# Attention into a GELU MLP on one core: weighted sums two units at a time, with 64-row products for the half blocks

## The chip, the cores and the metric

The kernel runs on one NeuronCore of one Trainium2 chip. The metric is the device time of one execution in microseconds (us); smaller is better. Engines are named as in the profile: PE is TensorE's matmul, PEld its weight load, DVE VectorE, ACT ScalarE, POOL GpSimd, SP the queue that issues the DMAs.

## The reference

Eight batches of eight heads, 576 positions of 64 features, with a causal window of 128 and a linear bias, followed by a two-layer MLP on the 4608 tokens:

```
scores = q @ k.T / sqrt(64) + bias        # (8, 8, 576, 576), only 0 <= i - j < 128 counts
attn   = softmax(scores)
x      = (attn @ v) as (4608, 512)        # "weighted sums"
out    = gelu(x @ w_in) @ w_out           # 512 -> 2048 -> 512, float32 result
```

Every matrix product keeps float32 precision by splitting each operand into two float16 parts (high and low) and adding three products: high*high, high*low, low*high.

## The kernel before

**Units.** The attention works on units: one batch `b` and one pair of heads `hp`, so 4 units a batch and 32 in all. A unit has 9 query blocks of 64 queries. Query block `j` sees the key blocks `j-2`, `j-1` and `j` (64 keys each, 192 keys).

**Stages of a unit.** `scores` (line 496) computes the scores with 54 products of 64 rows and 64 output rows; `biased` (548) scales them on DVE and adds the bias; `softmax` (633) takes maxima on DVE, exponentials on ACT and writes normalised weights (high part by POOL, low part by DVE in `low_weights`, 652) into the one buffer `e_main`; two transposing DMAs from SP's queue (line 658) turn them into the tile `et`, keys on partitions. `et` has two buffers, `et0` for units 0 and 2 and `et1` for units 1 and 3 of a batch.

**Weighted sums.** `weigh` (675) multiplies v by the weights. A 128-key block `kb` of v is the stationary operand (64 columns, one head), and `et` is the moving one, two query blocks (128 columns) at a time where both lie in the same part. For every even query block the block `kb = j/2` holds only 64 keys that count, and for every odd one the block `kb = (j-3)/2` does; the other 64 rows of such a product are zeros. Head 0 writes partitions 0 to 63 and head 1 partitions 64 to 127 of one PSUM bank, so two products stand side by side in the array. The MLP runs on tiles of 512 tokens, which don't end where batches end (576 tokens), so a unit's 9 query blocks fall into two parts (`blocks_of`, 670): part 0 goes to MLP tile `b`, part 1 to tile `b+1`, each in a bank of its own. `leave` (708) brings a part out of PSUM: ACT writes the high float16 part to the tile `x` (line 720), DVE the low part (line 721, shown as the helper's line 218).

**Order of the work.** The first three batches (0 to 2) follow an order written out by hand. Batches 3 to 7 are computed inside the loop over MLP tiles `t = 2` to 6 (line 1250), with `b = t + 1`. Each tile has 32 steps: in steps 0 to 15 `mlp_in` (12 products of 128x128 by 512 columns, line 747) and `gelu`, in steps 16 to 31 12 products of `mlp_out` (line 793) each, with `put` after every fourth. After these products a step may also start the scores of a unit (steps 2, 11, 16, 21) or weigh one (steps 12, 20, 30, 30):

```
SCORES_AT, WEIGH_AT = (2, 11, 16, 21), (12, 20, 30, 30)
```

In tile 2 the first scores come at step 4 and the first weighing at step 13; in tile 6 the last scores come at step 22. A scheduler that simulates the engines orders each engine's instructions from this program order; PE follows it in the trace.

**PSUM.** Eight banks: four under the tag `mm` (MLP products, and the score banks that begin with group 4 or 7) and four under `att` (the other three banks of a unit's scores, and the banks `av` of the weighted sums). A bank is reused once its readers on DVE and ACT are done.

## Time and profile before

| | us |
|---|---|
| median of 3 runs | 880.12 |
| lowest and highest of them | 879.17, 880.38 |
| the profiled execution | 879.11 |
| its span in the profile | 877.3 |

The profiled execution has its own time, and a span (first to last instruction) that is 1.8 us shorter. In the rows, a group of instructions has its line in the kernel, its engine, output and inputs, the shape (array rows * columns, then partitions x elements) and a count. In a timeline the first column is the start in us from the span's start, the second the time from the first start to the last end; since products overlap, the price of a group is better read from its start to the start of the next group.

### The profile page before, as it was taken

What the parts mean: (1) busy time and instruction counts of PE and PEld (TensorE: products, weight loads), DVE (VectorE), ACT (ScalarE), POOL (GpSimd) and SP (SyncE); (2) the same over time, 40 slices, a digit from 0 to 9 for tenths busy, and PEclk for the clock granted to TensorE, in tenths of its full rate; (3) what the DMA queues carried; (4) which work ended last, traced back from release to release, by engine and by line L of the source; (5) the groups of instructions that cost most, each with busy time, mean ns of one, the idle gap of its engine ahead of it and who ended that gap; (6) DMA issues with size and microseconds to landing.
All of it is one profiled execution on the core that took longest, in us unless ns stands there. A gap on an engine that the chain in (4) does not pass through costs nothing.

```text
span 877.3 us, 18582 instructions
## 1 busy us (share of the span) xinstructions
PE 861.7 (98%) x7428; PEld 476.9 (54%) x7428; DVE 709.3 (81%) x1388; ACT 546.5 (62%) x1147; POOL 196.0 (22%) x412
## 2 busy tenths in 40 slices
PE   6999999999999999999999999999999999999998
PEld 4644445544554545454545545445545554588887
DVE  6999999999768984887578775878477889998871
ACT  8999879896755573465464455466355338644760
POOL 0011000222015440452126421543054310000000
PEclk9999999999999999999999999999999999999999
DMA  9766645452572346233622473225122330001001
GB/s 311 268 208 230 228 117 133 134 168 62 132 233 38 73 97 203 57 69 77 187 72 56 93 171 117 55 55 118 39 56 56 78 67 13 0 13 37 1 1 49
DMA packets 174598, 91.63 MB, mean 104 GB/s; under 512 B 133680, under 2 KB 156336, under 8 KB 174384
## 3 DMA queue, kind: packets, MB, share of 16 engines
q1 hardware_dynamic: 174512, 90.45, 38.3%
q8 instruction: 58, 0.95, 0.4%
q14 instruction: 28, 0.23, 0.1%
HBM read 46.53 MB, written 9.44 MB: 64 GB/s over the span
## 4 chain that ended last, share of the span: by engine, by line
PE 70%; DVE 12%; ACT 2%; DMA 2%; issue 2%; POOL 1%; SPq 0%; ACTq 0%; POOLq 0%; DVEq 0%
PE h L747 27%; PE o L793 24%; PE av L700 4%; PE u_out L1082 4%; PE sc L529 3%; PE u L995 2%; DVE e_main L218 2%; DMA et<-e_main 2%; PE v L995 2%; DVE nmax L638 1%; DVE s L555 1%; PE z_out L1082 1%; PE x_out L1082 1%; PE y_out L1082 1%; PE v_out L1082 1%
## 5 line engine op out<-in xcount | busy, mean ns | idle before, releaser
L747 PE MATMUL h<-x,wi 128*128 128x512 f16 x1536 | 337.7, 379 | 1.1 <-ACT g L769 0.6
L747 PEld LDWEIGHTS <-wi 128*128 128x128 f16 x1536 | 148.5, 98 | 181.2 <-issue 4.0
L793 PE MATMUL o<-wo,g 128*128 128x512 f16 x864 | 192.4, 379 | 0.0
L793 PEld LDWEIGHTS <-g 128*128 128x128 f16 x1152 | 110.9, 98 | 132.8 <-issue 0.3
L641 ACT ACTIVATE s<-s,nmax 128x192 f32<-128x192 f32 x252 | 110.8, 441 | 46.3 <-DVE nmax L638 46.1
L218 DVE SCALAR_TENSOR_TENSOR e_main<-s,z,e_main 128x192 f16<-128x192 f32 x252 | 116.3, 505 | 15.2 <-POOL e_main L650 10.4
L771 POOL TENSOR_SCALAR g<-g,sg 128x512 f16<-128x512 f32 x96 | 76.8, 806 | 228.0 <-ACT g L769 200.8
L769 ACT ACTIVATE g<-h,gs 128x512 f32<-128x512 f32 x96 | 64.0, 686 | 95.9 <-PE h L747 59.1
L218 DVE SCALAR_TENSOR_TENSOR g<-g,sg,g 128x512 f16<-128x512 f32 x96 | 80.1, 851 | 34.0 <-POOL g L771 33.8
L650 POOL TENSOR_SCALAR e_main<-s,z 128x192 f16<-128x192 f32 x180 | 89.1, 514 | 66.9 <-ACT s L641 37.9
L555 DVE SCALAR_TENSOR_TENSOR s<-sc,cs,bias_h 128x384 f32<-128x384 f32 x112 | 64.2, 608 | 10.1 <-PE sc L529 9.9
L793 PE MATMUL o<-wo_first,g 128*128 128x512 f16 x288 | 65.9, 379 | 0.0
L720 ACT ACTIVATE x<-av,cx 128x448 f16<-128x448 f32 (+6 forms) x52 | 24.3, 481 | 62.0 <-PE av L700 59.5
L790 PE MATMUL o<-zo,g 128*128 128x512 f32 x128 | 57.0, 597 | 0.0
L638 DVE TENSOR_REDUCE nmax<-s 128x5 f32<-128x960 f32 (+1 forms) x56 | 56.6, 1043 | 0.4 <-POOL s L561 0.3
L529 PE MATMUL sc<-kbuf,qbuf 64*64 64x192 f16 (+3 forms) x1656 | 48.3, 250 | 7.6 <-ACT qbuf L431 4.4
L561 POOL MEMSET s<- 64x128 f32 (+1 forms) x112 | 19.2, 172 | 142.3 <-DVE s L555 131.2
L218 DVE SCALAR_TENSOR_TENSOR x<-av,cx,x 128x448 f16<-128x448 f32 (+6 forms) x52 | 24.7, 493 | 28.5 <-ACT x L720 28.4
L641 ACT ACTIVATION_READ_ACCUMULATOR s<-s,nmax 128x1 f32 x252 | 47.1, 187 | 0.0
L700 PEld LDWEIGHTS <-vbuf 128*64 128x64 f16 x1680 | 40.4, 111 | 9.4 <-issue 8.8
L700 PE MATMUL av<-et,vbuf 128*64 128x128 f16 (+1 forms) x1680 | 42.7, 210 | 0.4 <-DMA et<-e_main 0.3
L1082 PEld LDWEIGHTS <-g 128*128 128x128 f16 x384 | 37.6, 98 | 4.6
(269 smaller groups left out, 1126.3 us busy)
## 6 DMA issues: line engine op xcount, KB each, us to landing
v<-vp SPq DMA_DIRECT2D x32, 320.0 KB, 5.2
out<-ob SPq DMA_DIRECT2D x34, 256.0 KB, 2.2
raw<-w_in SPq DMA_DIRECT2D x8, 1024.0 KB, 11.0
raw<-w_out SPq DMA_DIRECT2D x8, 1024.0 KB, 6.7
q<-qp SPq DMA_DIRECT2D x7, 1152.0 KB, 6.0
k<-kp SPq DMA_DIRECT2D x7, 1152.0 KB, 7.5
qbuf<-qp SPq DMA_DIRECT2D x4, 288.0 KB, 5.4
kbuf<-kp SPq DMA_DIRECT2D x4, 288.0 KB, 5.7
```

The lines of the kernel that those rows point to most:

```text
L218: return nc.vector.scalar_tensor_tensor(out=dst, in0=src, scalar=scale, in1=high, op0=ALU.mult, op1=ALU.subtract)
L529: done = nc.tensor.matmul(ps[bank][o, n, gap:W], a, m[:, gap:W], start=(i == 0 and (n == 0 or b > 0)), stop=(i == len(terms) - 1 and b > 0 ...
L555: yield nc.vector.scalar_tensor_tensor(out=s[:, bank[0] : bank[0] + k, :], in0=ps[bank][:, 0:k, 0:W], scalar=cs, in1=bias.broadcast_to([P, ...
L638: yield nc.vector.tensor_reduce(out=nmax[:, r], in_=s[:, r], axis=AX.X, op=ALU.max, negate=True)
L641: yield nc.scalar.activation(s[:, i, :], s[:, i, :], AF.Exp, bias=nmax[:, i : i + 1], accum_out=z[:, i : i + 1])
L650: yield nc.gpsimd.tensor_scalar(e[:, i, 0, c], s[:, i], z[:, i : i + 1], 1.0, op0=ALU.mult, op1=ALU.mult)
L700: done = nc.tensor.matmul(av[r, (j - blocks[0]) * QB : (j - blocks[0] + len(js)) * QB], v32s[b][:, hp, kb, r] if b < EXACT else vbuf[:, vi ...
L747: done = nc.tensor.matmul(ph, wi[n][:, a, cc, k * P : (k + 1) * P], x[:, cc, b, :], start=(i == 0), stop=(i == 3 * NCC - 1),)
L769: yield nc.scalar.activation(g32, ph, AF.Gelu, scale=gsc[t, n])
L771: yield nc.gpsimd.tensor_scalar(g[:, r, 0], g32, gsg[t, n], 1.0, op0=ALU.mult, op1=ALU.mult)
L793: done = nc.tensor.matmul(o, g[:, r, a, c], wo[n][:, b, k, :], start=(fc == first and i == 0), stop=(fc == last and i == 2),)
L1082: nc.tensor.matmul(ps[name][:, tb], f(d, a)[:, k, tb * P : (tb + 1) * P], w(d, b, k), start=first, stop=True, skip_group_check=True,)
```

## The change

For batches 3 to 7, two units are weighed together: units 0 and 1 after step 18, units 2 and 3 after step 30 (no shift in tile 2 any more). `weigh_two` computes the half blocks as products of 64 rows, rows 0 to 63 for even query blocks (`low`) and rows 64 to 127 for odd ones (`high`), one query block (64 columns) a product, two `low` and two `high` in turn; then the whole 128-row blocks, again one query block a product. Even and odd query blocks of a part go to banks of their own, each bank holding both units: up to four `av` banks at once, from `att`. PE's order within it is fixed as written. `leave_two` brings out bank by bank: ACT both units in one instruction, DVE one instruction for each unit.

```diff
@@ new, beside weigh @@
+    def parity_blocks(b, part, odd):
+        return [j for j in blocks_of(b, part) if j % 2 == odd]
+
+    def weigh_two(one, two):
+        b, pair = one.b, (one, two)
+        k = 1 if b < EXACT else 2
+        banks = [(part, odd) for part in range(2) for odd in range(2) if parity_blocks(b, part, odd)]
+        for part, odd in banks:
+            one.av[part, odd] = bank_of([P, TT], "att" if b else "mm", f"av{one.u}_{b + part}_{odd}")
...
+        def job(rows, st, u, h, vi, ei, kb, slot, j):
+            part, odd, n = where[j]
+            g = 4 if j == 8 else (NEVEN if odd else 0) + 2 * h + j // 4
+            half = h if j == 8 else half_of(b, h, j)
+            c = slice(h * D, h * D + D)
+            at = (u * len(parity_blocks(b, part, odd)) + n) * QB
...
+                (part, odd, h), one.av[part, odd][c, at : at + QB],
+                v32s[b][rows, st.hp, kb, c] if b < EXACT else vbuf[rows, vi, st.hp, kb, c],
+                st.et[rows, (g * k + ei) * 2 + slot, half * QB : half * QB + QB],
...
+        terms = ((None, 0),) if b < EXACT else ((0, 0), (0, 1), (1, 0))
+        each = [(st, u, t) for u, st in enumerate(pair) for t in terms]
+        low = [(st, u, t, j // 2, 1, j) for st, u, t in each for j in range(0, NB, 2)]
+        high = [(st, u, t, (j - 3) // 2, 0, j) for st, u, t in each for j in range(3, NB, 2)]
+        for n, (st, u, t, *at) in enumerate(low):
+            for h in range(2):
+                job(slice(0, D), st, u, h, *t, *at)
+            if n < len(high):
+                st, u, t, *at = high[n]
+                for h in range(2):
+                    job(slice(D, P), st, u, h, *t, *at)
+        for st, u, t in each:
+            for j in range(1, NB):
+                for h in range(2):
+                    job(slice(0, P), st, u, h, *t, (j - 1) // 2, j % 2, j)
...
+            done = nc.tensor.matmul(o, a, m, start=key not in started, stop=left[key] == 0, skip_group_check=True)
...
+    def leave_two(one, two):
...
+        for part in range(2):
+            t = b + part
+            for odd in range(2):
+                js = parity_blocks(b, part, odd)
...
+                av = one.av[part, odd][:, 0 : 2 * n * QB].rearrange("p (u n k) -> p u n k", u=2, n=n)
...
+                yield nc.scalar.activation(dst(0, (0, 1)), av, AF.Copy, scale=c)
+                for u in range(2):
+                    yield low_part(dst(1, (u,)), av[:, u], c, dst(0, (u,)))
@@ the loop over tiles @@
-    SCORES_AT, WEIGH_AT = (2, 11, 16, 21), (12, 20, 30, 30)
+    SCORES_AT, WEIGH_AT = (2, 11, 16, 21), (18, 30)
...
-            scores_at[0], weigh_at[0] = scores_at[0] + 2, weigh_at[0] + 1
+            scores_at[0] += 2
...
-            for hp in range(NPAIR):
-                if weigh_at[hp] == step:
-                    for part in range(2):
-                        run(weigh(unit(b, hp), [part]))
-                        run(leave(unit(b, hp), [part]))
+            if step in WEIGH_AT:
+                two = [unit(b, 2 * WEIGH_AT.index(step) + n) for n in range(2)]
+                with tc.manual_schedule(engines={mybir.EngineType.PE}):
+                    run(weigh_two(*two))
+                run(leave_two(*two))
```

## Rows read from the trace of the kernel before

**Rows 1.** The page's busy times: PE, share of the span, instructions.

```profile
PE 861.7 (98%) x7428; PEld 476.9 (54%) x7428; DVE 709.3 (81%) x1388; ACT 546.5 (62%) x1147; POOL 196.0 (22%) x412
```

**Rows 2.** Stretches: one MLP tile (t = 3); columns: length, busy us by engine, PEclk.

```profile
344.60:438.86 94.26, 94.26 (x818) 46.89 (x817) 70.98 (x151) 50.33 (x112) 33.02 (x68) 1.00 0.42 101
```

**Rows 3.** Waits of PE, 250 to 725 us: total, times, longest.

```profile
PE h L747 <- ACT g L769: 0.6, 1, 0.6
```

**Rows 4.** Timeline of PE, batches 3 and 4: start, length, group, count.

```profile
310.00 1.60 PE L700 MATMUL av<-et,vbuf 128*64 128x128 f16 x66
311.53 2.76 PE L793 MATMUL o<-wo,g 128*128 128x512 f16 x12
...
339.06 3.00 PE L700 MATMUL av<-et,vbuf 128*64 128x128 f16 x132
342.00 2.76 PE L793 MATMUL o<-wo,g 128*128 128x512 f16 x12
...
380.99 1.55 PE L700 MATMUL av<-et,vbuf 128*64 128x128 f16 x54
382.47 7.94 PE L747 MATMUL h<-x,wi 128*128 128x512 f16 x36
...
417.77 7.93 PE L793 MATMUL o<-wo,g 128*128 128x512 f16 x36
...
428.13 5.34 PE L793 MATMUL o<-wo,g 128*128 128x512 f16 x24
433.41 2.91 PE L700 MATMUL av<-et,vbuf 128*64 128x128 f16 x108
436.25 2.76 PE L793 MATMUL o<-wo,g 128*128 128x512 f16 x12
```

**Rows 5.** Line 700's products, 309.9 to 311.5 and 380.9 to 382.4, by shape.

```profile
L700 PE MATMUL av<-et,vbuf x66: 192/196/243, 310.0 to 311.4; 128*64 128x64 f16 x36, 128*64 128x128 f16 x30
...
L700 PE MATMUL av<-et,vbuf x54: 192/219/243, 381.0 to 382.3; 128*64 128x128 f16 x42, 128*64 128x64 f16 x12
```

**Rows 6.** Weight loads begun by 433.43, 433.45 (line 700); 446.74, 446.76 (line 529).

```profile
433.41 0.11 PEld L700 LDWEIGHTS <-vbuf 128*64 128x64 f16 x2 [0.42 <-issue]
...
433.41 0.14 PEld L700 LDWEIGHTS <-vbuf 128*64 128x64 f16 x4 [0.42 <-issue]
...
446.72 0.11 PEld L529 LDWEIGHTS <-qbuf 64*64 64x64 f16 x4 [0.42 <-issue]
...
446.72 0.14 PEld L529 LDWEIGHTS <-qbuf 64*64 64x64 f16 x8 [0.42 <-issue]
```

**Rows 7.** Line 700 in its densest stretch (batch 1): length, PE, PEld with counts.

```profile
142.20:143.69 1.49, 1.49 (x86) 1.49 (x82) 1.00 0.04 11
```

**Rows 8.** Batch 5 around step 18: PE, DVE, second unit's last transposing DMA, third's.

```profile
488.45 7.94 PE L793 MATMUL o<-wo,g 128*128 128x512 f16 x36
...
488.70 0.60 DVE L218 SCALAR_TENSOR_TENSOR x<-av,cx,x 128x384 f16<-128x384 f32 x1
...
491.65 1.13 DVE L555 SCALAR_TENSOR_TENSOR s<-sc,cs,bias_h 128x384 f32<-128x384 f32 x2
...
L658 SPq DMA_TRANSPOSE et<-e_main x1: 1589/1589/1589, 487.7 to 487.7; - x1
...
DMA to landing us min/median/max: 3.7/3.7/3.7
...
L658 SPq DMA_TRANSPOSE et<-e_main x1: 2421/2421/2421, 500.0 to 500.0; - x1
```

**Rows 9.** Batch 3 around step 18: PE (steps 17 on) and DVE.

```profile
299.54 6.65 PE L793 MATMUL o<-wo,g 128*128 128x512 f16 x30
...
304.12 1.13 DVE L555 SCALAR_TENSOR_TENSOR s<-sc,cs,bias_h 128x384 f32<-128x384 f32 x2
```

**Rows 10.** DVE groups of line 721 (helper line 218), 250 to 725 us.

```profile
L218 DVE SCALAR_TENSOR_TENSOR x<-av,cx,x 128x256 f16<-128x256 f32 x8 | 3.8, 477 | 6.5 <-ACT x L720 6.4
...
L218 DVE SCALAR_TENSOR_TENSOR x<-av,cx,x 128x128 f16<-128x128 f32 x4 | 1.4, 342 | 6.0 <-ACT x L720 6.0
```

## The prediction

> **What bounds the kernel now.** I read the busy times first, then the stretches, then the waits, then the timeline. PE is busy 98% of the span [rows 1]. [...] Between 250 and 725 us, which is where the change acts, PE waited once, for 0.6 us [rows 3]. So in this stretch a microsecond taken from PE's own work is a microsecond of the result, and DVE has some 23 us of slack a tile, though not at every moment. The question is what PE pays for the weighted sums now and what it pays after.

> **Prices from the timeline.** From a group's start to the next group's start, a unit of batch 3 takes 311.53 - 310.00 = 1.53 us and two in a row 342.00 - 339.06 = 2.94; a unit of batch 4 takes 1.48, two 2.84 [rows 4]. Heads 0 and 1 run side by side, so I count pairs of products. The unit of 1.53 has 36 products of 64 columns and 30 of 128, thus 18 and 15 pairs; the other has 12 and 42, thus 6 and 21 [rows 5]. With a for a pair of 64 columns, b for one of 128 and f for what a group pays once, the second unit of a double group gives 18a + 15b = 2.94 - 1.53 = 1.41 and 6a + 21b = 2.84 - 1.48 = 1.36. Three times the second less the first: 48b = 2.67, so b = 0.0556 us, a = (1.41 - 0.83) / 18 = 0.032 us and f = 1.53 - 1.41 = 0.12 us. Entering a group costs a little more, ahead of its start: 48 products of the MLP take 428.13 - 417.77 = 10.36 us, 24 take 5.18, but the group at 433.41 begins 5.28 after 428.13 [rows 4], so 0.10.

> **Before, batches 3 to 7.** Batches 3 and 5 have two single groups and a double one: 1.53 + 1.53 + 2.94 + 3 x 0.10 = 6.30. Batches 4 and 6: 1.48 + 1.48 + 2.84 + 0.30 = 6.10. Batch 7 splits into parts otherwise, 12 pairs of 64 and 18 of 128 a unit: 12a + 18b = 1.39, so 1.51 + 1.51 + 2.90 + 0.30 = 6.22. In all 2 x 6.30 + 2 x 6.10 + 6.22 = 31.0 us.

> **After.** A group of two units has 2 units x 3 terms = 6 rounds over the blocks. Low half blocks (j = 0, 2, 4, 6, 8): 30 pairs. High ones (3, 5, 7): 18 pairs. Whole blocks (1 to 8): 48 pairs. All have 64 columns, 192 products and as many weight loads. The gain is in the 18 high pairs, which use the rows that the low ones leave free.
> - Whole blocks: 48a = 1.54 us, a form that the trace has.
> - Half blocks: no row shows four products of 64 columns at once. [...] So 30a = 0.96.
> - Entry 0.10, f 0.12, and one more change of tile form, from 64 to 128 rows, inside the group. No row shows that one; I take f, 0.12, with 0.02 and 0.22 as its ends.

> Sum 0.10 + 0.96 + 0.12 + 1.54 + 0.12 = 2.84 us a group, ten groups 28.4: **PE saves 2.6 us**. The five groups fewer (15 become 10), with their entries and exits, are in that already. The ends for the inner change of form are worth 1 us over ten groups either way.

> **What lies beside it.** ACT brings out the same columns in as many instructions, four for a pair of units. DVE needs eight where four did: by 342 ns for 128 columns and 477 for 256 [rows 10] an instruction costs some 0.21 us whatever its width, so 4 x 0.21 = 0.8 us more a pair, 1.7 a batch. The slack of 23 us a tile covers it; the price, if it doesn't, is a bank that comes free late.

> **The moved steps.** Units 0 and 1 are weighed after step 18 rather than 12 and 20.
> - Their weights must have landed. In batch 5 the second unit's last transposing DMA is issued at 487.7 and lands 3.7 later, at 491.4 [rows 8]. PE ends step 18 at 488.45 + 2 x 2.59 = 493.6, less the 1.53 of unit 0 that no longer come first: 492.1. Slack 0.7.
> - All four banks of `att` are wanted, and three hold the third unit's scores until DVE's fourth bias operation, 491.65 + 0.57 = 492.2 [rows 8]; the piece of `x` ahead of it (0.60 at 488.70) is gone, so 491.6. Slack 0.5. In batch 3, PE comes at 299.54 + 5.18 - 1.53 = 303.2 and the banks at 304.12 + 0.57 = 304.7 [rows 9], less the two pieces of `x` that are gone from DVE's queue, about 1.0 us by [rows 10]: 303.7, a wait of 0.5; none if the work behind them, which waited for POOL too, moves up further.
> - `et0` is free for unit 2 only after step 18. SP stands in that transposing DMA anyway: in batch 5 the first is issued at 500.0 [rows 8], after the group's end near 495. So nothing behind it on SP (the `put` of step 19) is held longer.
> - The scores of unit 3, at step 21, need three banks back. PE gives 3 x 2.59 = 7.8 us for four ACT and eight DVE pieces (3 us of DVE), which stand among unit 2's softmax on the same queues. Likely enough, not certain.
> - Step 30: the next tile reads `x` of units 2 and 3 after 12 products of step 31 and 6 of its own, 3.9 us; the two banks of part 0 that it reads need four pieces of DVE, 1.4 us, close behind ACT's two. Without that cover each late microsecond would be PE's.

> I put 0.1 us of wait on each batch, 0.5 in all (0 to 1.3 is plain): 2.6 - 0.5 = **2.1 us saved**. The profiled execution of 879.11 would become 877.0. It stands 1.0 below the median of the runs, 880.12, so I predict 880.12 - 2.1 = **878.0 us**, 876.3 to 879.5 for this case with the ends above. About 0.2%, 1.8 us, is what a measurement of this kernel tells from no change.

> **Rivals.**
> - *PE can't be fed.* 384 instructions in 2.84 us are 7.4 ns each. The densest long stretch has 168 in 1.49 us, 8.9 ns [rows 7], and the double group of batch 3 has 264 in 2.94, 11.1 ns [rows 4]. Both are explained by a and b, so they are no limits shown; but nothing shows that 7.4 can be held. At 8.9 ns a group takes 3.42, at 11.1 it takes 4.27: 5.8 to 14.3 us more over ten, less the 2.6, so 883 to 892 us. It decides from 31.0 / 10 / 384 = 8.1 ns on: slower. Chance 0.18.
>   [...]
> - *The row halves don't run at once*, so the change doesn't do what it says: 18 more rounds of 0.032, 0.58 a group, 5.8 in all, less 2.6: 883.3 us. Against it speak the loads [rows 6]. Chance 0.08.
> - *Waits give it back.* DVE's bias operations or its eight pieces come late at step 18 or 21, PE waits 0.2 to 0.6 us a batch (to 3.0 over five): 878.5 to 880.5, no change that can be told. For it speak the slacks of 0.5 and less. Chance 0.24.
> - *As forecast.* Chance 0.50; in 0.43 of it the waits stay under 0.8 us and the gain over 1.8.

> **How the numbers follow.** Faster: 0.43. Within 0.2%: 0.07 of the forecast's case and 0.22 of the third rival's, 0.29. Slower: 0.18 + 0.08, and 0.02 where waits exceed the gain, 0.28. The range runs from 876.3 (under it 0.07: no waits and a cheap change of form) to 886 (over it 0.12: most of the fed-too-slowly case past 9.5 ns).

> **What would show it.** Right: groups of line 700's successor of 2.7 to 2.8 us from start to the next group's start, low and high products beginning within a few ns of each other at rounds near 32 ns, PE still without waits over 0.5 us at steps 18 and 21. Wrong: gaps in the middle of a group with no releaser (feeding), rounds of 64 ns (row halves in turn), or waits of PE for DVE's bias operations or pieces of `x`. A gain far beyond 3 us would mean that PE's work elsewhere moved too.

## The result, and the profile after

The changed kernel takes 884.13 us in the median of 6 runs (882.25 to 885.78), the kernel before 879.67 beside it: 1.0051 times as long, 95% interval 1.0037 to 1.0064. It is slower by 4.5 us where 2.1 less had been forecast. The profiled execution took 883.97 with a span of 882.1, 4.8 more than the 877.3 of before. Of all the runs below, two were disturbed and stand in no ratio: one of g_dve_pieces (904.78 us) and one of the kernel before beside h_old7_only and i_terms_old7 (3181.88).

From the page after: busy times (share of the span, instructions), the queue that fetches instructions (packets, MB, share), and the chain that ended last by engine.

```profile
PE 862.9 (98%) x8148; PEld 477.4 (54%) x8148; DVE 719.8 (82%) x1424; ACT 542.5 (61%) x1145; POOL 198.5 (23%) x412
...
q8 instruction: 64, 1.05, 0.5%
...
PE 62%; DVE 19%; ACT 3%; issue 3%; POOL 1%; DMA 1%; SPq 0%; POOLq 0%; ACTq 0%; DVEq 0%
```

The same two lines of before, which were not among its rows:

```profile
q8 instruction: 58, 0.95, 0.4%
...
PE 70%; DVE 12%; ACT 2%; DMA 2%; issue 2%; POOL 1%; SPq 0%; ACTq 0%; POOLq 0%; DVEq 0%
```

PE is as busy as before by its share [rows 1], with 720 products and 720 loads more. DVE takes a larger part of the chain. Each fetch brings 1.05 / 64 MB = 16.4 KB in both kernels. PE's products and loads, 14856 of them before and 16296 after, are 256 and 255 a fetch.

PE's waits after, 245 to 730 us (total, times, longest), where before had one of 0.6 [rows 3]:

```profile
PE av L754 <- issue: 2.7, 2, 1.6
PE h L822 <- DVE x L218: 0.8, 1, 0.8
PE h L822 <- ACT g L844: 0.6, 1, 0.6
```

"Issue" is idle time for which the profile has no releaser. Line 754 is the new form's product, 822 and 868 are the MLP's. The timeline of PE after shows a group that ran freely and the tile start behind it, and then batch 5's two groups:

```profile
339.01 2.78 PE L754 MATMUL av<-et,vbuf 64*64 64x64 f16 x192
341.73 2.76 PE L868 MATMUL o<-wo,g 128*128 128x512 f16 x12
344.32 5.34 PE L822 MATMUL h<-x,wi 128*128 128x512 f16 x24
349.60 0.54 PE L529 MATMUL sc<-kbuf,qbuf 64*64 64x192 f16 x10
350.07 2.76 PE L822 MATMUL h<-x,wi 128*128 128x512 f16 x12
352.77 1.17 PE L529 MATMUL sc<-kbuf,qbuf 64*64 64x192 f16 x44
353.88 4.49 PE L822 MATMUL h<-x,wi 128*128 128x512 f16 x20
...
492.19 2.49 PE L754 MATMUL av<-et,vbuf 64*64 64x64 f16 x173
495.77 0.50 PE L754 MATMUL av<-et,vbuf 128*64 128x64 f16 x19 [1.10 <-issue]
496.21 2.76 PE L868 MATMUL o<-wo,g 128*128 128x512 f16 x12
...
528.70 2.40 PE L754 MATMUL av<-et,vbuf 64*64 64x64 f16 x167
532.70 0.60 PE L754 MATMUL av<-et,vbuf 128*64 128x64 f16 x25 [1.60 <-issue]
533.23 2.76 PE L868 MATMUL o<-wo,g 128*128 128x512 f16 x12
```

Three readings.

- **The free group costs what was forecast**: 341.73 - 339.01 = 2.72 us, against 2.74 without its entry. Seven of the ten groups take 2.71 to 2.79.
- **Batch 5's groups stop**: 496.21 - 492.19 = 4.02 and 533.23 - 528.70 = 4.53 us, 1.31 and 1.82 more, the first after 173 products (346 instructions), the second after 167 (334).
- **The next tile's first scores are cut in two** (10 and 44 products). From the MLP's start through the last of these scores, 36 products and 54, it takes 353.88 - 344.32 = 9.56 us. The same stretch of before, which isn't among its rows:

```profile
344.60 7.93 PE L747 MATMUL h<-x,wi 128*128 128x512 f16 x36
352.46 1.28 PE L529 MATMUL sc<-kbuf,qbuf 64*64 64x192 f16 x54
353.67 4.71 PE L747 MATMUL h<-x,wi 128*128 128x512 f16 x21
```

There it took 353.67 - 344.60 = 9.07, so the cut costs 0.49 us.

The profile doesn't print where a block of PE's program begins, but it can be counted whether the two stops stand at one place of such a grid. From the start of the group at 492.19 to that of the one at 528.70 PE has 780 products and loads, 12 more than three blocks of 256, and the second group stops 12 instructions earlier. With the grid laid so that both stops are a block's first instructions, blocks begin, to within a few instructions, at the 88th and 344th instruction of the first and at the 76th and 332nd of the second. One other group also has two, at its 8th and 264th, the one at 398.05; it didn't stop, and lost 0.08 us behind its 38th product, where no block begins. The instruction queue in the stretch just before that group (395.0 to 398.05), and inside the one at 492.19 (493.3 to 495.7):

```profile
q8 instruction: 1, 0.02, 2.0%
...
q8 instruction: 1, 0.02, 2.9%
```

In the harmless case the next block was fetched from 395.34 to 396.29, ahead of the group; at 492.19 only from 493.44 to 494.55, well inside it, and PE resumed at 495.77. That the late block is what stops PE is a reading so far; e2_shift_good and e2_shift_bad below test it. The block of 256 instructions is an estimate from the 256 and 255 instructions a fetch; at the pace of a free group (2.71 us) one runs through in 256 x 2.71 / 384 = 1.81 us. At 492.19 the fetch itself took 1.11 us, and PE resumed 1.22 us after its end.

What happens behind the group at 528.70, in the timeline of ACT and DVE:

```profile
533.08 2.43 ACT L421 ACTIVATE vbuf<-v,scv 128x2560 f16<-128x2560 f32 x1 [14.71 <-PE av L754]
...
535.42 1.65 ACT L779 ACTIVATE x<-av,cx 128x128 f16<-128x128 f32 x4
535.54 2.88 DVE L218 SCALAR_TENSOR_TENSOR vbuf<-v,scv,vbuf 128x2560 f16<-128x2560 f32 x1 [12.00 <-ACT vbuf L421]
...
538.35 2.29 DVE L218 SCALAR_TENSOR_TENSOR x<-av,cx,x 128x64 f16<-128x64 f32 x8
```

ACT first splits the next batch's v (line 421, 2.43 us) and only then brings out `x` (line 779); DVE's `x` pieces come after its own part of v. A reason is this, and e1_terms tests it below. Of the three terms, (0, 0), (0, 1), (1, 0), the last reads v's low part, so the high part, which ACT overwrites, comes free before the banks are complete.

**The last stage.** Behind batch 7, DVE works through one chain that ends near 808 us in before. The rows below take that chain from the end of one short gap in DVE's work to the start of another at its end; columns: stretch, length, busy us (instructions) of PE, PEld, DVE, ACT and POOL, clock, DMA. First before, then after:

```profile
705.10:807.80 102.70, 102.57 (x782) 67.38 (x781) 98.95 (x154) 55.99 (x94) 4.29 (x9) 1.00 0.11 28
```

```profile
708.50:812.60 104.10, 101.75 (x850) 66.85 (x849) 99.43 (x156) 55.47 (x93) 4.29 (x9) 1.00 0.12 28
```

In before, PE and DVE are both all but full, and the chain that ended last stays on PE until 804.1 us; in the changed kernel it leaves PE at 667.0, in tile 6, and from there runs through DVE for the most part. After, the stretch begins 3.4 us later and is 1.4 longer: 3.4 + 1.4 = 4.8, the whole of the difference. DVE is busy 0.48 longer in it and idle 0.92 longer (4.67 against 3.75). DVE's timeline, before and then after:

```profile
723.30 0.74 DVE L218 SCALAR_TENSOR_TENSOR x<-av,cxl,x 128x512 f16<-128x512 f32 x1
...
726.56 0.75 DVE L218 SCALAR_TENSOR_TENSOR x<-av,cxl,x 128x512 f16<-128x512 f32 x1
...
756.53 1.42 DVE L218 SCALAR_TENSOR_TENSOR g<-room_s,sg,g 128x512 f16<-128x512 f32 x2 [1.49 <-ACT g L932]
```

```profile
727.72 2.50 DVE L966 TENSOR_TENSOR vbuf<-room,vbuf 128x512 f16<-128x512 f32 x4 [0.61 <-ACT vbuf L965]
...
731.27 1.65 DVE L218 SCALAR_TENSOR_TENSOR x<-av,cxl,x 128x256 f16<-128x256 f32 x4
...
761.29 1.41 DVE L218 SCALAR_TENSOR_TENSOR g<-room_s,sg,g 128x512 f16<-128x512 f32 x2 [1.76 <-ACT g L1007]
```

Four pieces of 256 columns stand where two of 512 did. A wait of 0.61 for ACT is new, and the gap before the two pieces of `g` grows from 1.49 to 1.76, by 0.27: 0.88 of the 0.92.

DVE falls behind in tile 6 already. Two operations of it there, before and then after:

```profile
687.74 2.49 DVE L882 TENSOR_TENSOR room<-wo_first 128x1024 f32<-128x1024 f16 x2
...
696.98 0.69 DVE L891 TENSOR_TENSOR qbuf<-room,qbuf 128x512 f16<-128x512 f32 x1 [0.74 <-ACT qbuf L890]
```

```profile
689.87 2.49 DVE L957 TENSOR_TENSOR room<-wo_first 128x1024 f32<-128x1024 f16 x2
...
694.92 1.65 DVE L218 SCALAR_TENSOR_TENSOR x<-av,cxl,x 128x256 f16<-128x256 f32 x4
...
700.38 0.69 DVE L966 TENSOR_TENSOR qbuf<-room,qbuf 128x512 f16<-128x512 f32 x1 [0.74 <-ACT qbuf L965]
```

The first is 2.1 us later than before, the second 3.4. Between them DVE now brings out `x` for both units of batch 7's first group (1.65 us and 0.46 in smaller pieces), where before had one unit's (0.74 and 0.27). From the one to the other it takes 9.24 us in before and 10.51 after; d_move_only takes 9.74 (686.47 to 696.21), so the move makes 0.5 of the 1.3 and the new form the rest.

### The profile page after: what moved, and what is told of

The parts are those of the page before. It is cut to its first block, busy times and chain, and to the rows that moved or that the text cites. A ratio compares the mean times of both kernels' runs of the same rounds, so it can differ in the third digit from the quotient of the medians.

```text
span 882.1 us, 20059 instructions
## 1 busy us (share of the span) xinstructions
PE 862.9 (98%) x8148; PEld 477.4 (54%) x8148; DVE 719.8 (82%) x1424; ACT 542.5 (61%) x1145; POOL 198.5 (23%) x412
## 3 DMA queue, kind: packets, MB, share of 16 engines
q8 instruction: 64, 1.05, 0.5%
## 4 chain that ended last, share of the span: by engine, by line
PE 62%; DVE 19%; ACT 3%; issue 3%; POOL 1%; DMA 1%; SPq 0%; POOLq 0%; ACTq 0%; DVEq 0%
PE h L822 25%; PE o L868 18%; PE o L865 5%; DVE e_main L218 3%; PE sc L529 3%; PE av L754 3%; DVE g L218 3%; PE u L1070 2%; PE u_out L1157 2%; DVE s L555 2%; PE v L1070 1%; ACT s L641 1%; DVE nmax L638 1%; DMA et<-e_main 1%; PE av L700 1%
## 5 line engine op out<-in xcount | busy, mean ns | idle before, releaser
L846 POOL TENSOR_SCALAR g<-g,sg 128x512 f16<-128x512 f32 x96 | 78.9, 830 | 224.3 <-ACT g L844 223.3
L218 DVE SCALAR_TENSOR_TENSOR g<-g,sg,g 128x512 f16<-128x512 f32 x96 | 85.8, 915 | 31.1 <-POOL g L846 30.9
L218 DVE SCALAR_TENSOR_TENSOR vbuf<-v,scv,vbuf 128x2560 f16<-128x2560 f32 x7 | 20.2, 2886 | 37.3 <-ACT vbuf L421 37.3
L421 ACT ACTIVATE vbuf<-v,scv 128x2560 f16<-128x2560 f32 x7 | 17.0, 2427 | 41.6 <-PE av L754 41.6
L529 PEld LDWEIGHTS <-qbuf 64*64 64x64 f16 x1512 | 30.9, 107 | 16.1 <-issue 13.7
L865 PEld LDWEIGHTS o<-zo,g 128*128 128x128 f32 x128 | 23.8, 190 | 27.5 <-issue 25.8
```

The lines of the kernel that those rows point to most:

```text
L218: return nc.vector.scalar_tensor_tensor(out=dst, in0=src, scalar=scale, in1=high, op0=ALU.mult, op1=ALU.subtract)
L529: done = nc.tensor.matmul(ps[bank][o, n, gap:W], a, m[:, gap:W], start=(i == 0 and (n == 0 or b > 0)), stop=(i == len(terms) - 1 and b > 0 ...
L846: yield nc.gpsimd.tensor_scalar(g[:, r, 0], g32, gsg[t, n], 1.0, op0=ALU.mult, op1=ALU.mult)
L865: done = nc.tensor.matmul(o, g[:, r, c], zo[n][:, n % 2, k * DM : (k + 1) * DM], start=(fc == first), stop=(fc == last))
```

## The experiments

Ratios are to the kernel before on the same chip (medians 879.7 to 880.0 there), with 95% intervals. g_again, run once, took 880.70 us. Times are compared by these medians and traces stage by stage: up to 288 us all but e2_shift_bad have the same order of PE's products, yet the traces used here already differ by up to 2 us in that part (PE's 2000th product begins between 245.5 and 247.6 us; 246.2 in before, 246.3 after).

| run | us | runs | ratio, interval |
|---|---|---|---|
| as changed | 884.13 | 6 | 1.0051 (1.0037 to 1.0064) |
| e2_shift_bad | 894.95 | 4 | 1.0173 (1.0156 to 1.0189) |
| e2_shift_good | 883.46 | 4 | 1.0038 (1.0023 to 1.0053) |
| d_move_only | 878.57 | 10 | 0.9986 (0.9976 to 0.9995) |
| e1_terms | 881.59 | 10 | 1.0018 (1.0009 to 1.0028) |
| e3_both | 881.90 | 6 | 1.0028 (1.0016 to 1.0039) |
| e4_both_old7 | 877.35 | 9 | 0.9977 (0.9967 to 0.9986) |
| g_dve_pieces | 880.56 | 11 | 1.0011 (1.0001 to 1.0020) |
| h_old7_only | 882.91 | 6 | 1.0032 (1.0021 to 1.0044) |
| i_terms_old7 | 880.62 | 11 | 1.0012 (1.0003 to 1.0021) |

**Where the blocks begin** (e2_shift_good, e2_shift_bad). Some MLP products are done as two of 256 columns. That adds instructions ahead of the groups and moves the block starts; the weighted sums are untouched. The badly placed kernel has the entry 2: 48 as well, so that blocks begin in every group where they do in batch 5's.

```diff
+    PADS = {3: 40, 4: 40, 5: 40, 6: 40}
-                done = nc.tensor.matmul(ph, ...)
+                split = i > 0 and padded.get(t, 0) < PADS.get(t, 0) and fc > 1
+                padded[t] = padded.get(t, 0) + split
+                for c in (slice(0, HT), slice(HT, TT)) if split else (slice(0, TT),):
+                    done = nc.tensor.matmul(ph[:, c], ...)
```

> The changed kernel with 40 MLP products a tile (tiles 3 to 6) issued as two of 256 columns, 80 more PE instructions a tile that cost PE about 0.1 us; they only move where the 256-instruction blocks of PE's program begin within the ten weighing groups, to instructions 184 and 172 of each. Theory (a group stalls when two block beginnings fall inside its 384 instructions, since the second block is not there in time): the stalls of 1.3 and 1.8 us in batch 5 are gone and none comes, the groups take 2.71 us, 881.0 us in all. Rival (the stalls are DMA traffic or another event of that moment): they stay where they are, 884 us.

> As the run before, with 48 products of tile 2 split as well, so that a block begins at instruction 88 or 76 of every group and the next one inside it too. Theory: all ten groups stall for 1.2 to 1.8 us before their last 20 to 26 pairs, eight more than in the changed kernel, about 12 us more of PE time; the end comes at 894 to 897 us. Rival (not the blocks): no new stalls, 884 us.

PE's waits over the whole span, placed badly:

```profile
PE av L754 <- issue: 13.4, 10, 1.6
```

and its timeline at batch 3's second group, which ran freely in the changed kernel:

```profile
340.57 2.40 PE L754 MATMUL av<-et,vbuf 64*64 64x64 f16 x167
344.59 0.60 PE L754 MATMUL av<-et,vbuf 128*64 128x64 f16 x25 [1.62 <-issue]
345.12 2.76 PE L872 MATMUL o<-wo,g 128*128 128x512 f16 x12
```

It now takes 345.12 - 340.57 = 4.55 us and stops after 167 products, as batch 5's did. All ten groups stop, and the time is 894.95. Placed well, none stops; batch 5's second group and PE's largest wait behind it:

```profile
528.24 2.78 PE L754 MATMUL av<-et,vbuf 64*64 64x64 f16 x192
530.95 2.76 PE L872 MATMUL o<-wo,g 128*128 128x512 f16 x12
```

```profile
PE h L826 <- ACT room L1041: 3.1, 1, 3.1
```

It is 2.71 us again. The same 192 products with the same data thus run with or without the stop, by their place in the program alone: shown by both runs. Yet the time fell by only 0.7 us, within the intervals: this program's order in tile 7 differs, and PE waits 3.1 us for ACT there, a wait that the changed kernel doesn't have (its own wait for ACT, further on at line 1070, is 1.6 us). So the time of this run alone doesn't price the stops.

**The move without the new form** (d_move_only). The old products at the new places.

```diff
-    SCORES_AT, WEIGH_AT = (2, 11, 16, 21), (12, 20, 30, 30)
+    SCORES_AT, WEIGH_AT = (2, 11, 16, 21), (18, 18, 30, 30)
-            scores_at[0], weigh_at[0] = scores_at[0] + 2, weigh_at[0] + 1
+            scores_at[0] += 2
```

> The kernel before with its own products and banks, only weighed at the changed kernel's places (units 0 and 1 after step 18, units 2 and 3 after step 30). Theory (moving costs nothing, and ten double groups save five entries of PE, 0.2 us each): 878.5 to 880 us, no stalls of PE above 0.5 us. Rival (the moved steps make the loss: weights, banks or x late): 882 us or more, with waits of PE at steps 18 and 21 or at the tile starts.

It took 878.57, 1.4 us under before, with no wait of PE over 0.6 us between 245 and 730 us. Two single groups and their entries, 1.53 + 1.53 + 0.20, become 2.94 + 0.10, which is 0.22 a batch and 1.1 in five: over a third of the forecast's gain is the move's own. Of the waits priced at 0.5 us it has 0.2, for `x` at tile 7's start.

**The order of the terms** (e1_terms).

```diff
-        terms = ((None, 0),) if b < EXACT else ((0, 0), (0, 1), (1, 0))
+        terms = ((None, 0),) if b < EXACT else ((1, 0), (0, 0), (0, 1))
```

> Only the order of the three terms in the paired weighing is changed, so that the high part of v is read last and the next batch's conversion of v can't start before the last bank is finished. Theory (the loss has three parts: instruction blocks that come late inside a group, about 3.1 us in batch 5; bringing out the sums behind the conversion of v, which splits the next tile's first scores in two, about 1.9 us over four tiles; and a DVE chain that passes every delay on to the end): the scores of units 0 are in one piece again, the 0.3 to 0.6 us at each tile start are gone, the two stalls of 1.3 and 1.8 us in batch 5 stay, 882.2 us. Rival (the extra DVE instructions or the dense groups themselves make the loss, the order costs nothing): 884.0 us, within 0.5 of the changed kernel.

ACT and DVE behind batch 5's second group in this kernel:

```profile
533.87 1.67 ACT L779 ACTIVATE x<-av,cx 128x128 f16<-128x128 f32 x4 [15.01 <-PE av L754]
534.26 2.29 DVE L218 SCALAR_TENSOR_TENSOR x<-av,cx,x 128x64 f16<-128x64 f32 x8 [10.23 <-ACT x L779]
535.41 2.44 ACT L421 ACTIVATE vbuf<-v,scv 128x2560 f16<-128x2560 f32 x1
```

`x` now comes first, the scores of the next tiles are whole again, the 0.8 us of tile 7's start is gone, and the time is 2.5 us under the changed kernel's. Batch 5's stops remain (PE waits 3.0 us for issue in all).

**Both repairs** (e3_both: the terms' order and the well-placed blocks).

> Both repairs of PE's path together: the order of terms of e1_terms and the block positions of e2_shift_good. Theory (PE's saving is real, some 2.4 us by the last scores of batch 7, but from there on a gapless chain on DVE sets the end, and the paired weighing of batch 7 adds four DVE instructions, 0.8 us, and a wait of 0.6 to that chain): no stall and no split group, DVE's chain after 704 us starts some 2.2 us earlier than in the kernel before, and the end is only about 1 us earlier, 879.0 us. Rival (PE alone sets the end): 877.3 us. Rival (the simulated order of tile 7 gets worse as in e2_shift_good, whatever PE does): 881 us or more, with PE waiting for ACT in tile 7.

881.90: the expected 879 was missed, and the rival of a poorer order in tile 7 came true. All groups run without a stop, but tile 7 keeps waits that belong to neither repair: 2.4 us for ACT (line 1041) and 0.8 for `x`. Both lie behind batch 7's groups, so the new form there was suspected next.

**Both repairs, and batch 7 in the old form** (e4_both_old7).

```diff
+            for hp in range(NPAIR if b == B - 1 else 0):
+                if (18, 18, 30, 30)[hp] == step:
+                    for part in range(2):
+                        run(weigh(unit(b, hp), [part]))
+                        run(leave(unit(b, hp), [part]))
-            if step in WEIGH_AT:
+            if step in WEIGH_AT and b < B - 1:
```

> As e3_both, but batch 7, whose sums come out just ahead of the last stage, keeps the products, banks and single pieces of the kernel before (units 0 and 1 after step 18, 2 and 3 after step 30). Theory: PE gives 0.4 us back, DVE's chain loses the four extra instructions and the wait, 877.7 us, clearly faster than the kernel before. Rival (DVE's pieces in batch 7 don't matter): the same as e3_both or 0.4 slower.

877.35, 2.4 us under before, and the fastest of all. It is 1.2 under the move alone, though the two intervals overlap. The timelines bear it out: double groups of the old form take 2.85 to 2.94 us in d_move_only and the new ones 2.71 here, which is 0.14 to 0.23 a group over the eight groups of batches 3 to 6. The last stage's stretch of this kernel has before's length and DVE's busy time:

```profile
703.20:805.90 102.70, 102.37 (x780) 67.19 (x779) 98.95 (x153) 56.01 (x93) 4.29 (x9) 1.00 0.10 28
```

**More DVE instructions in the kernel before** (g_dve_pieces, and the same kernel again as g_again, whose trace is used): the low parts of batch 7's units 2 and 3 in four pieces each.

```diff
-            yield low_part(x[:, 1], av[:, :n], c, x[:, 0])
+            pieces_ = 4 if b == B - 1 and hp >= 2 else 1
+            for k in range(pieces_):
+                r = slice(k * n // pieces_, (k + 1) * n // pieces_)
+                yield low_part(x[:, 1, r], av[:, r], c, x[:, 0, r])
```

> The kernel before; only the low parts of units 2 and 3 of batch 7 are taken out in four pieces each instead of one, 12 more DVE instructions, about 2.5 us of DVE work ahead of the last stage and nothing else. Theory (DVE's chain from 705 us on has no slack and sets the end): 882.0 to 882.5 us, PE waiting that much longer near 805 us. Rival (DVE has slack there, PE sets the end): within 0.5 us of the kernel before, 879.9.

> A second look at the kernel before with twelve more DVE instructions in batch 7's units 2 and 3, for its trace. Time as measured there, 880 to 881. If DVE's chain sets the end and the pieces were only smaller than thought, the stretch from 705 us to the end of the chain is longer by what the twelve cost (12 times some 0.1) and the gaps in it stay; if the pieces fell into idle time of DVE, the sum of gaps in that stretch shrinks by what they cost and its end stays.

Only 0.8 us came where 2.5 was expected; 880.56 lies between what the theory and the rival gave. The stretch in g_again:

```profile
705.80:809.40 103.60, 102.73 (x783) 67.39 (x782) 100.35 (x166) 55.76 (x94) 4.30 (x9) 1.00 0.11 28
```

The twelve instructions cost DVE 100.35 - 98.95 = 1.4 us, not 2.5, and the stretch grew by 0.9: one gap in it shrank from 0.79 to 0.30. So what DVE gets to do here lengthens the end, less what fits into gaps. That is the chain's mechanism, at about two thirds of the price.

**One repair or none, with batch 7 in the old form** (h_old7_only: the changed kernel but for batch 7; i_terms_old7: with the terms' order as well).

> The changed kernel with one thing undone: batch 7 is weighed in the old form (at the moved places 18, 18, 30, 30); batches 3 to 6 keep the new form, the old order of terms and the block stalls of batch 5. Theory (the last stage's chain of DVE pieces adds its own 1.3 to 1.5 us, beside what PE brings late into tile 7): 882.7 us, 1.4 below the changed kernel. Rival (batch 7's form costs nothing of its own; only PE's lateness counts): 884.0. Second rival (old form in batch 7 also lifts the scheduler's poorer order of tile 7's start): 881.5 or less.

> Terms in the order that reads v's high part last, and batch 7 in the old form; nothing done about the block starts, so the two stalls of batch 5 (3.4 us together) should be there. Theory: 881.6 of the run with the terms alone, less 1.4 for batch 7 = 880.2, and 877.4 of the kernel with all three repairs plus 3.4 of stalls, less the 0.56 that batch 7's second group stalled = 880.2 to 880.8 as well: the parts add. Rival (the stalls are hidden again by the last stage's chain, which has no room for them only because PE is late): near 878.5.

882.91 and 880.62, both where the theory put them. Each is 1.0 to 1.2 us under the run that differs from it by batch 7's form alone (the changed kernel and e1_terms), with intervals that overlap, so this part is likely rather than shown. i's trace still has the two stops, and e4, which differs from i only in the split products that move the blocks, is 3.3 us faster, clear of the intervals: here, where nothing else changed in tile 7, the stops are priced.

```profile
PE av L754 <- issue: 3.3, 2, 1.7
```

## Why the prediction was wrong

By its own steps.

- **The products: right.** The sum without entry was 2.74 us a group, and 2.71 was measured; no row of before shows a round of four 64-row products, and giving it the 0.032 us of a pair, 0.96 for 30 rounds, was the author's estimate; in the group at 339.01 such rounds come every 32 ns (40 products in 0.32 us), the starts of all 30 rounds lie within 0.95 us, and the inner change of form takes 0.12 from the last 64-row product's start to the first 128-row one's, a little less than was taken. The rival in which the row halves don't run at once is refuted.
- **"PE can't be fed": half right as a rival, and at nothing in the forecast's sum.** Its sign, a gap in the middle of a group with no releaser, came in two of ten groups. It asked, though, whether 7.4 ns an instruction can be held, and over the 384 of a group it can: 2.71 / 384 = 7.1 ns. That 884 lies in its 883 to 892 is luck, since less than half of what was lost is of this kind. What fails is the arrival of the next block of program when 256 instructions pass in 1.8 us and the next block was not fetched ahead of the group, as it was for the group at 398.05. It cost 1.31 + 1.82 = 3.1 us in batch 5, and by place alone it could have cost nothing or ten times 1.4 to 1.8 us (e2_shift_good, e2_shift_bad). Before's own groups of 264 instructions in 2.94 us [rows 4] are too short to hold two block starts unless one falls on their first instructions.
- **"Step 30": failed.** The 3.9 us of cover were to hide four pieces of DVE "close behind ACT's two". The working left out who else wants ACT: the split of v, 2.43 us on ACT and 2.88 on DVE, which the term order releases first. The next tile's scores are cut in two, 0.5 us at tile 3 by the rows above and 1.75 over the four tiles 3 to 6 read in the same way, and at tile 7's start PE waits 0.8. Putting the low part's term first (e1_terms) took 2.5 us off.
- **The eight DVE pieces, "the slack of 23 us a tile covers it": failed in batch 7.** The 23 us of slack, 94.26 - 70.98, is that of a middle tile [rows 2]. In the last stage DVE is busy 98.95 of 102.70 us, and with the new pieces and the wait beside them it takes 1.4 longer. Old form in batch 7 alone gives 1.2 back (h_old7_only), 1.0 with the terms' order (i against e1_terms), each at the edge of the noise; g_again shows that added DVE work there does lengthen the end. In tile 6 the pieces of both units, moved and in the new form, make DVE 1.3 later.
- **The waits at steps 18 and 21 (0.5 us)** were about right: one wait, in batch 3 and for DVE's bias operation, where the prediction had placed it. That group takes 3.25 us, 0.5 more than a free one; batches 4 to 7 have no such wait over 0.2.

The account has two parts. Up to tile 7 it is PE's: 1.31 + 1.82 of stops, 0.1 + 0.5 in two other groups and 1.75 at the tile starts are 5.5 us, and the groups save 31.0 - 10 x (2.71 + 0.10) = 2.9. The difference of 2.6 stands against 724.30 - 721.89 = 2.4, by which PE enters tile 7 later (before, then after):

```profile
721.89 6.44 PE L747 MATMUL h<-x,wi 128*128 128x512 f16 x29
```

```profile
724.30 1.89 PE L822 MATMUL h<-x,wi 128*128 128x512 f16 x8
726.97 4.26 PE L822 MATMUL h<-x,wi 128*128 128x512 f16 x19 [0.78 <-DVE x L218]
```

From there on DVE's chain sets the end: 2.1 us late in tile 6 at 689.87, 1.3 more by 700.38 and 1.4 more in the last stage are the 4.8 between the spans. PE's wait of 0.78 for `x` is this chain seen from PE and isn't added to it. By the runs, the terms' order is worth 2.5 us (e1_terms), batch 7's form then 1.0 (i_terms_old7) and the place of the blocks then 3.3 (e4_both_old7).

Two things stay open. The time from entering a block to the use of the next one was not measured by itself; the 1.81 us of a block and the stop behind it give an estimate of 3.1 to 3.6 us. And why the padded programs get a poorer order in tile 7 as long as batch 7 has the new form is the scheduler's doing and was not followed; that old form there removes it is shown (e3_both against e4_both_old7).

## What to carry to other kernels

A group of very short instructions has to be checked against where the program's blocks begin, not only against the rate: here 256 instructions pass in 1.81 us, less than the 3.1 to 3.6 us estimated from one block's start to the use of the next, and two block starts inside a group of 384 stopped PE in all ten groups of e2_shift_bad; with the starts moved by 96 instructions none of ten stopped (e2_shift_good). When an operand's high and low parts are read in turn, the order of the terms decides which buffer comes free first, and with it what the engines behind do first: 2.5 us here (e1_terms). Slack has to be read from the stage in which the added work lands: here DVE was idle for 23 us of a middle tile's 94.26 and for 3.75 of the last stage's 102.70.
